# A gated attention and GLU mix in split fp32: one stock of buffers, and a new seam between its two phases

## The chip, the core and the metric

The kernel is one program on one core of a Trainium2 chip. The metric is the device time of one execution in microseconds (us), as the median of several runs; lower is better. The engines that matter are TensorE (PE in the profile, with its weight loads as PEld), VectorE (DVE), ScalarE (ACT), GpSimd (POOL, which here issues DMAs that add to what lies in the target) and SyncE (SP, which issues the plain DMAs).

## The reference, cut to what matters

x has 2048 rows of 512 columns. A sigmoid gate per row mixes two branches: linear attention with 32 heads of 16, and a bilinear GLU with 1792 hidden columns. All of it is fp32.

```
x = A_x                                              # [2048, 512]
g = sigmoid((x * gate_w).sum(-1))                    # one number per row
q, k, v = split(x @ wqkv);  phi(t) = where(t > 0, t + 1, exp(t)) + 1e-6
kv  = einsum("bhsd,bhse->bhde", phi(k), v);  z = phi(k).sum(over rows)
num = einsum("bhqd,bhde->bhqe", phi(q), kv)
den = einsum("bhqd,bhd->bhq", phi(q), z) + 1e-6
a = (num / den) @ wo
b = ((x @ w_gate) * (x @ w_up)) @ w_down
out = g * a + (1 - g) * b
```

## The kernel before, in words

**Arithmetic.** Every fp32 operand is held as two parts, a high one in the type fp32r and a low one (operand minus high). A product is three matmuls, high by high, high by low and low by high (`mm3`, L72). The high part is a copy on ACT, the low part a subtraction on DVE.

**Phase 1** (L171 to L348) goes over 16 tiles of 128 rows. For a tile t it computes k (12 matmuls into the bank `pk`), phi(k) on ACT and DVE (`phi_k`, `phi_split`), splits x (`split_x`, which also sums x times `gate_w` into a column of `scol`), and adds x-transposed times phi(k) into four banks `gt` (12 matmuls, `g_unit`), four tiles behind the k products. So the loop has 12 turns with both kinds of products and, at its end, four with g products alone. The sum over rows of phi(k) gathers in `zacc`. After the last turn come the gates: a sigmoid on a 128 x 16 column tile gives `gcol` (g) and `ocol` (1 - g), which two DMAs write to DRAM in turned order, one element at a time (L341), and from where they are read later as rows: g by eight loads (`g2_load`, L767), 1 - g in the last group of each half (`row`, L498). In this phase the loop also loads and splits the sums of x blocks that phase 2 needs (`cb_load`), and the weights of the first units. Its buffers come from a pool of its own (`p1`), with a fixed count for each kind.

**Phase 2** works on two halves of 1024 rows (`pair`). A half has 16 **units** of seven products each: two q units and 14 f units (gate and up columns of the GLU). A unit multiplies four weight blocks by blocks of x with seven products in place of eight: sums of weight blocks and sums of x blocks are formed first, and the seven results are combined through four PSUM banks Y, X, R, S by ACT and DVE (`crit`, L599). One product is six matmuls of 512 columns. It has a **slot**: slot 7n+s is the product s of unit n, and everything else is put down against slots (`later(slot, fn)`). Two f units make a **group** (7 per half). Beginning 11 slots after its first one, a group's products with w_down run as 14 **jobs** of three matmuls each, one to a slot, behind the unit's product. They run in banks `pdn`, of which there are four, and are gathered in SBUF tiles `M`: every other job has its bank loaded beforehand with the old sum by ACT (`seed`) and evacuated by ACT, the rest are added by DVE. The last group of a half is plain, and its jobs and the attention's last products run in `turn` behind the half's last unit, and in the first slots of the next half (`FILL`).

**Weights.** `w_load(n)` loads five of a unit's seven weight blocks (640 KB) by SP when the unit n-3 is emitted; `w_add(n)` fills the last two from the first two with the sign turned, on ACT, and then a DMA of POOL adds five more blocks to blocks 2 to 6; `w_high` and `w_low` split the result. `d_load`, `d_add`, `d_high` and `d_low` do the same for a group's w_down. The ACT copy in `w_add` and `d_add` waits for the load, and what stands behind it on ACT waits with it.

**The seam.** At the end of phase 1 SP has, in order, the two gate stores, eight loads for attention (`wp_load`: w_v and w_o, 256 KB each), the eight g loads, and only then the first w_down load. Of the units the q ones come first, at slots 0 to 13. The term kv is made at slot 9 (`kv_unit`) from the `gt` banks, which ACT and DVE have copied out ahead of slot 0 (`g_evac`).

**Order.** Every instruction is pinned in the order in which the code emits it, engine by engine. An engine, SP and POOL too, takes its instructions in that order and holds at the first whose wait isn't over. Phase 2's 512-column tiles come from one stock of 45 buffers (`get`, L357, takes the one that was given back longest ago; `put` gives back).

Of the kernel before, what the change touches and what calls it, by code (L numbers as in the profile page):

```python
# [7 lines left out]
F32 = mybir.dt.float32  # L8
# [6 lines left out]
P = 128  # L15
S = 2048
D = 512
# [18 lines left out]
SLOT = {3: 0, 4: 1, 5: 2, 2: 3, 1: 4, 6: 5, 7: 6}  # L36
# [5 lines left out]
def gated_mix(ctx: ExitStack, tc, xt, xp, x, wqkv, wq, wq_add, wo, wgu, wgu_add, wdn, wdn_add, gate_w, out):  # L42
# [48 lines left out]
    gcol = const.tile([P, NT], F32, name="gcol")  # L91
    ocol = const.tile([P, NT], F32, name="ocol")
# [24 lines left out]
    gates = [dram.tile([NT, P], F32, name=f"gate{v}") for v in "go"]  # L117


    order = [("q", j) for j in range(2)] + [("f", f) for f in range(NF)]  # L120
    units = len(order)
    order = [(pair, *u) for pair in range(NPAIR) for u in order]
# [4 lines left out]
    def w_load(n):  # L127

        if n < len(order):
            _, kind, m = order[n]  # L130
            raws[n] = const.tile([P, 7, 2 * P], F32, tag="wr", name="wr", bufs=2)
            dma(raws[n][:, 0:5], (wgu if kind == "f" else wq)[m])

    def w_add(n):

        if n < len(order):
            _, kind, m = order[n]
            act(raws[n][:, 5:7], raws[n][:, 0:2], scale=-1.0)
            dma_add(raws[n][:, 2:7], (wgu_add if kind == "f" else wq_add)[m])

    PARTS = ((0, 2), (2, 4), (4, 7))
# [27 lines left out]


    accs = [psum.tile([P, D], F32, tag="pd", name=f"gt{d}", bufs=4) for d in range(KT)]  # L171
    with tc.tile_pool(name="p1", bufs=2, reuse_waits="tile") as p1:

        warm = psum.tile([P, CH], F32, tag="Y", name="warm")
        for _ in range(WARM):
            mm(warm, zeros[:, :P], zeros, start=True, stop=True)
        gw = p1.tile([P, D], F32, name="gw", bufs=1)
        zacc = p1.tile([P, D], F32, name="zacc", bufs=1)
        nc.vector.memset(zacc, 0.0)
        wkh = p1.tile([P, KT, D], F32R, name="wkh", bufs=1)  # L180
        wkl = p1.tile([P, KT, D], F32R, name="wkl", bufs=1)

        xop = {}
        for t in range(2 * CH // P):
            c, i = divmod(t, CH // P)
            xop[t] = [part[:, :, i * P:(i + 1) * P] for part in (xa, xb)[c]]


        raw_of = [p1.tile([P, D], F32, tag="raw", name="wraw", bufs=4) for _ in range(KT)]

        def raw_load(k, by):
            pin(by.dma_start(raw_of[k], wqkv[k * P:(k + 1) * P, D:2 * D]))

        raw_load(0, nc.scalar)
        for k in range(KT):
            raw = raw_of[k]
            a = p1.tile([P, LEAD, P], F32, tag="xtraw", name="xlead", bufs=4)
            step = LEAD // 2 if k == 0 else LEAD
            for i in range(0, LEAD, step):
                sl = slice(i * P, (i + step) * P)  # L200
                dma(a[:, i:i + step].rearrange("p t c -> p (t c)"), xp[0, A1 + k // 2][:, k % 2, sl])
                if i + step == LEAD and k + 1 < KT:
                    raw_load(k + 1, nc.sync)
                if i == 0:
                    act(wkh[:, k], raw)
                split(xa[0][:, k, sl], xa[1][:, k, sl], a[:, i:i + step].rearrange("p t c -> p (t c)"), "dve")
                if i == 0:
                    tt(wkl[:, k], raw, wkh[:, k].bitcast(F32), ALU.subtract)

        xs, xts, pks = {}, {}, {}  # L210

        def load_x(t):
            xs[t] = p1.tile([P, D], F32, tag="raw", name="xraw", bufs=4)
            dma(xs[t], x[t * P:(t + 1) * P, :])

        def load_xt(t):
            xts[t] = p1.tile([P, KT, P], F32, tag="xtraw", name="xtraw", bufs=4)
            dma(xts[t], xt[t])

        def split_xt(t):  # L220
            if t not in xop:
                xop[t] = [p1.tile([P, KT, P], F32R, tag=f"xt{v}", name=f"xt{v}", bufs=3) for v in "hl"]
            split(*xop[t], xts.pop(t))

        def k_mm(pk, t, k, **kw):
            mm3(pk, [v[:, k] for v in xop[t]], (wkh[:, k], wkl[:, k]), k == 0, k == KT - 1, late=1, **kw)

        def phi_k(t, pk):

            e = p1.tile([P, D], F32, tag="e", name="e")  # L230
            r = p1.tile([P, D], F32, tag="u", name="r")
            act(e, pk, AF.Exp)
            act(r, pk, AF.Relu)
            ph = p1.tile([P, D], F32, tag="ph", name="ph")
            stt(ph, e, 1.0, r, ALU.min, ALU.add)
            return t, ph

        def phi_split(t, ph):
            pkh = p1.tile([P, D], F32R, tag="pkh", name="pkh", bufs=4)
            pkl = p1.tile([P, D], F32R, tag="pkl", name="pkl", bufs=4)  # L240
# [23 lines left out]
        for t in range(1, 3):  # L264
            load_x(t)
            load_xt(LEAD + t)
# [752 lines left out]
```

## Time and profile before

| | |
|---|---|
| median of 3 runs | 643.28 us (642.03 to 646.67) |
| profiled execution, its own time | 644.63 us |
| its span, first to last instruction | 642.8 us |
| PE busy | 596.3 us (93%), 2579 matmuls |
| DVE busy | 507.0 us (79%) |
| ACT busy | 398.2 us (62%) |
| POOL busy | 57.0 us (9%) |
| moved by DMA | 107.35 MB, 167 GB/s on average |

A line of the profile that groups instructions gives the line of code, the engine, the operation, the tile written and those read, and the count. `L50` is the line of every matmul, `L56` of every ACT operation that goes through `act`, `L59` and `L62` of DVE's, `L80` of SP's DMAs and `L83` of POOL's, so tiles tell them apart. The chain of waits is followed back from the last instruction to what released each step. A row of the view by windows gives a stretch of time, its length, and for PE, PEld, DVE, ACT and POOL the busy time and the count of instructions, then the TensorE clock that was granted, the busy share of the DMA engines and their rate.

### The profile page before, as it was taken

Reading aid. Unit: us, or ns where it says so; the run is one execution under the profiler, and the core shown is the slowest. Engines: PE = TensorE matmul, PEld = TensorE weight load, DVE = VectorE, ACT = ScalarE, POOL = GpSimd, SP = SyncE. Lnnn points to the kernel's source line nnn. Section 1 sums busy time; section 2 is a strip of 40 time slices with the busy share of each in tenths; the row PEclk is TensorE's granted clock in tenths of the full one; section 3 lists DMA queues with packets and bytes.
Section 4 is the critical chain, followed back from the end, with each engine's and each line's share of the span. In section 5 each row is a group of like instructions: output and inputs, shape, how many; then the busy total and the mean of one; then the engine's idle time right before and its main releaser. Section 6 shows DMA issues by size and latency. Waiting matters only on the chain.

```text
span 642.8 us, 7716 instructions
## 1 busy us (share of the span) xinstructions
PE 596.3 (93%) x2579; PEld 483.4 (75%) x2579; DVE 507.0 (79%) x813; ACT 398.2 (62%) x707; POOL 57.0 (9%) x74
## 2 busy tenths in 40 slices
PE   8999995089799899999999879999999999999997
PEld 6888884078578688878887768867878888888776
DVE  6977874048699698988898885699989888889881
ACT  3756743159468587777776265666867777677410
POOL 0011100000101111112100011000101010000000
PEclk9999999589999899999999999999999999999999
DMA  8576928769967778889757626898757375660011
GB/s 296 184 198 163 256 42 36 226 132 285 255 153 217 156 221 202 216 200 229 180 140 238 214 68 150 227 248 210 209 141 164 91 158 140 144 139 19 0 66 66
DMA packets 46680, 107.35 MB, mean 167 GB/s; under 512 B 8080, under 2 KB 17296, under 8 KB 46608
## 3 DMA queue, kind: packets, MB, share of 16 engines
q1 hardware_dynamic: 37360, 70.41, 35.0%
q0 software_dynamic: 9136, 36.18, 30.2%
q8 instruction: 20, 0.33, 0.2%
q10 hardware_dynamic: 144, 0.26, 0.1%
q14 instruction: 20, 0.16, 0.1%
HBM read 95.55 MB, written 12.34 MB: 168 GB/s over the span
## 4 chain that ended last, share of the span: by engine, by line
PE 64%; DMA 17%; DVE 12%; ACT 3%; issue 3%; SPq 0%; DVEq 0%; ACTq 0%; POOL 0%; POOLq 0%
PE pdn L50 18%; PE bY L50 10%; PE bR L50 9%; PE bX L50 8%; PE pk L50 7%; PE gt L50 6%; PE bS L50 5%; DMA dr<-in_wdn 5%; DVE M L59 4%; DMA wr<-in_wgu 4%; DMA gateo<-ocol 3%; DMA xw<-in_xp 2%; DMA wo_sb<-in_wo 2%; DMA wr<-in_wgu_add 1%; DVE wcl L59 1%
## 5 line engine op out<-in xcount | busy, mean ns | idle before, releaser
L56 ACT ACTIVATE M<-pdn 128x512 f32<-128x512 f32 x98 | 58.6, 598 | 38.4 <-PE pdn L50 35.6
L50 PE MATMUL pdn<-hh,dh 128*128 128x512 f32 x200 | 78.4, 392 | 4.4 <-ACT pdn L56 4.4
L50 PE MATMUL pdn<-hl,dh 128*128 128x512 f32 x200 | 78.5, 393 | 3.6 <-DVE hl L59 3.6
L59 DVE TENSOR_TENSOR M<-M,pdn 128x512 f32<-128x512 f32 x86 | 58.9, 685 | 26.5 <-PE pdn L50 26.4
L50 PE MATMUL pdn<-hh,dl 128*128 128x512 f32 x200 | 78.3, 392 | 0.0
L59 DVE TENSOR_TENSOR wcl<-wr,wch 128x512 fp32r<-128x512 f32 (+1 forms) x96 | 74.3, 775 | 1.8 <-ACT wch L56 1.7
L56 ACT ACTIVATE wch<-wr 128x512 fp32r<-128x512 f32 (+1 forms) x96 | 66.9, 701 | 2.0 <-DMA wr<-in_wgu_add 1.9
L50 PE MATMUL bX<-xbh,wch 128*128 128x512 f32 x128 | 49.9, 390 | 0.0
L50 PE MATMUL bX<-xbh,wcl 128*128 128x512 f32 x128 | 49.8, 389 | 0.0
L50 PE MATMUL bX<-xbl,wch 128*128 128x512 f32 x128 | 49.8, 389 | 0.0
L83 POOL DMA_DIRECT2D wr<-in_wgu_add x28 | 24.7, 881 | 273.3 <-ACT wr L56 125.1
L50 PEld LDWEIGHTS pdn<-hh,dh 128*128 128x128 f32 x200 | 37.7, 188 | 13.4 <-ACT pdn L56 5.6
L50 PEld LDWEIGHTS pdn<-hl,dh 128*128 128x128 f32 x200 | 37.8, 189 | 12.5 <-DVE hl L59 4.8
L50 PE MATMUL bY<-xc4h,wch 128*128 128x512 f32 x64 | 26.4, 412 | 22.2 <-ACT m L56 22.2
L59 DVE TENSOR_TENSOR bR<-bX,m 128x512 f32<-128x512 f32 x32 | 22.3, 696 | 29.5 <-ACT m L56 21.9
L50 PEld LDWEIGHTS pdn<-hh,dl 128*128 128x128 f32 x200 | 37.7, 188 | 7.8
L56 ACT ACTIVATE pdn<-M 128x512 f32<-128x512 f32 x70 | 41.7, 596 | 0.0
L56 ACT ACTIVATE hh<-c 128x512 fp32r<-128x512 f32 x56 | 35.1, 626 | 9.2 <-DVE c L59 9.2
L59 DVE TENSOR_TENSOR hl<-c,hh 128x512 fp32r<-128x512 f32 x56 | 38.4, 686 | 2.5 <-ACT hh L56 2.4
L59 DVE TENSOR_TENSOR t<-bR,c 128x512 f32<-128x512 f32 x32 | 22.0, 687 | 17.3 <-PE bR L50 13.5
L56 ACT ACTIVATE c<-bX 128x512 f32<-128x512 f32 x28 | 16.8, 598 | 28.2 <-DVE bS L59 26.8
L50 PEld LDWEIGHTS bY<-xc4h,wch 128*128 128x128 f32 x64 | 12.5, 196 | 26.5 <-ACT m L56 24.0
(178 smaller groups left out, 1554.7 us busy)
## 6 DMA issues: line engine op xcount, KB each, us to landing
wr<-in_wgu SPq DMA_DIRECT2D x28, 640.0 KB
wr<-in_wgu_add POOLq DMA_DIRECT2D x28, 640.0 KB, 7.8
dr<-in_wdn SPq DMA_DIRECT2D x14, 640.0 KB
dr<-in_wdn_add POOLq DMA_DIRECT2D x12, 640.0 KB, 9.0
xraw<-in_x SPq DMA_DIRECT2D x16, 256.0 KB
terms<-zq SPq DMA_DIRECT2D x16, 256.0 KB
zt<-terms SPq DMA_DIRECT2D x16, 256.0 KB
rb<-den SPq DMA_DIRECT2D x16, 256.0 KB
```

What stands on the lines that cost most here:

```text
L50: tc.keep_in_program_order(nc.tensor.matmul(*args, **kw))
L56: pin(nc.scalar.activation(dst, src, func, **kw))
L59: pin(nc.vector.tensor_tensor(dst, a, b, op=op))
L83: tc.keep_in_program_order(nc.gpsimd.dma_start(dst, src, accum_op=ALU.add))
```

## The change

- **One stock.** Phase 1 takes all its tiles from the stock of 45 that phase 2 uses, and its pool is gone. The x block sums are loaded, added to and split in halves of 512 columns (ten in place of five), and from tile 4 on in place of tile 6.
- **The last g products.** The loop ends with tile 15's k products. The 16 pieces of three matmuls that remain (`g_piece`, tiles 12 to 15) stand in a queue, from which slots 0 to 13 take one each, slots 3 and 9 two. What they need (phi of the last two tiles, three splits of x), the sum of `zacc` and the gates are put down at slots 0 to 9. `g_evac` moves to slot 15, `kv_unit` from 9 to 16.
- **The gates.** g and 1 - g stand in one tile of 32 columns, which DVE turns in blocks of 32 x 32; four DMAs store rows of 32 elements.
- **The q units.** The second one comes behind the first group: q0, f0, f1, q1, f2 and so on. Its chain for the denominators has slots of its own (`ZAT`).
- **The weights.** A load brings three blocks (384 KB) in place of five. ACT fills four more with two copies, one with the sign turned and one of block 11 twice, and POOL's DMA adds five blocks as before. The plain group's w_down has a load of its own with four blocks. The order of blocks and parts changes with it.
- **SP's order at the seam.** The first w_down load goes ahead of the loads for attention, which go to slot 4; the g loads go to slot 14. The x sums of the second half start at slot 51 in place of 40 and hold their buffers for 10 slots in place of 15.

In the rows below, `wr` is a unit's raw weights, `dr` a group's, `wv` and `wo_sb` the attention's, `xraw` a tile of x, `terms` and `zt` what the denominators write and read, `g_` the g rows. SP at the seam, before:

```order
L80 DMA wr<-in_wgu 128x1280
L80 DMA gateg<-gcol 128x16x1
L80 DMA gateo<-ocol 128x16x1
L80 DMA wv<-in_wqkv 128x512 x4
L80 DMA wo_sb<-in_wo 128x512 x4
L80 DMA g_982<-gateg 32x1x128 x8
L80 DMA dr<-in_wdn 128x1280
L80 DMA wr<-in_wgu 128x1280
L80 DMA terms_1007<-zq 128x4x128 x4
```

And SP at the same place in the changed kernel:

```order
L80 DMA wr<-in_wgu 128x768
L80 DMA xraw<-in_x 128x512
L80 DMA dr<-in_wdn 128x768
L80 DMA wv<-in_wqkv 128x512 x4
L80 DMA wo_sb<-in_wo 128x512 x4
L80 DMA wr<-in_wq 128x768
L80 DMA terms_897<-zq 128x4x128 x2
L80 DMA gates<-turned 32x32 x4
L80 DMA terms_897<-zq 128x4x128 x2
L80 DMA wr<-in_wgu 128x768
L80 DMA g_896<-gates 32x1x128 x8
L80 DMA zt<-terms_897 128x512 x4
```

The first `dr` load stood behind both gate stores and the eight g loads, and stands ahead of them now; the weight rows are 768 elements wide in place of 1280.

PE where the units begin, before (`gt` the g banks, `pz` the sum of `zacc`, `bY` and `bX` a unit's banks):

```order
L50 MATMUL gt_92<-pkh,xnh 128x512
L50 MATMUL gt_92<-pkl,xnh 128x512
L50 MATMUL gt_92<-pkh,xnl 128x512
L50 MATMUL pz<-ones,zacc 128x2 x4
L50 MATMUL bY<-xah,wch 128x512
L50 MATMUL bY<-xal,wch 128x512
L50 MATMUL bY<-xah,wcl 128x512
```

PE between the first two products of the first unit, in the changed kernel:

```order
L50 MATMUL bY<-xah,wch 128x512
L50 MATMUL bY<-xal,wch 128x512
L50 MATMUL bY<-xah,wcl 128x512
L50 MATMUL gt_90<-pkh,xnh 128x512
L50 MATMUL gt_90<-pkl,xnh 128x512
L50 MATMUL gt_90<-pkh,xnl 128x512
L50 MATMUL bX<-xbh,wch 128x512
```

A g piece stands between two products where there was none; PE has 2535 rows in both programs.

ACT in an f unit of the dense part, around the fill of a unit's raw weights, before (`pdn<-M` is a seed):

```order
L56 ACTIVATE wch<-wr 128x768
L56 ACTIVATE wr<-wr 128x512
L56 ACTIVATE M<-pdn 128x512
L56 ACTIVATE xw<-xw 128x512
L56 ACTIVATE wch<-wr 128x512
L56 ACTIVATE pdn<-M 128x512
```

And in the changed kernel:

```order
L56 ACTIVATE xw<-xw 128x512
L56 ACTIVATE wr<-wr 128x512 x2
L56 ACTIVATE pdn<-M 128x512
L56 ACTIVATE wch<-wr 128x512
L56 ACTIVATE c_2203<-bX 128x512
```

The fill is two instructions in place of one, ahead of the next seed.

The diff, cut to its core:

```diff
-SLOT = {3: 0, 4: 1, 5: 2, 2: 3, 1: 4, 6: 5, 7: 6}
+SLOT = {3: 0, 4: 1, 2: 2, 6: 3, 7: 4, 5: 5, 1: 6}
...
-    order = [("q", j) for j in range(2)] + [("f", f) for f in range(NF)]
+    order = [("f", f) for f in range(NF)]
+    for j, place in enumerate((0, 3)):
+        order.insert(place, ("q", j))
...
-            dma(raws[n][:, 0:5], (wgu if kind == "f" else wq)[m])
+            dma(raws[n][:, 0:3], (wgu if kind == "f" else wq)[m])
+
+    def copies(raw):
+
+        act(raw[:, 3:5], raw[:, 0:2], scale=-1.0)
+        act(raw[:, 5:7], raw[:, 0:1].to_broadcast([P, 2, 2 * P]))
...
-            act(raws[n][:, 5:7], raws[n][:, 0:2], scale=-1.0)
+            copies(raws[n])
             dma_add(raws[n][:, 2:7], (wgu_add if kind == "f" else wq_add)[m])
 
-    PARTS = ((0, 2), (2, 4), (4, 7))
+    PARTS = ((0, 3), (5, 7), (3, 5))
...
-        for there, col in zip(gates, (gcol, ocol)):
-            dma(there.rearrange("t p -> p t"), col)
+        pin(nc.vector.transpose(rows, both))
+        for a in range(0, P, 2 * NT):
+            dma(gates[:, a:a + 2 * NT], rows[a:a + 2 * NT])
...
+    later(0, phi_rest)
+    later(2, phi_rest)
+    for t, s in zip(range(NT - LEAD + 1, NT), (1, 4, 7)):
+        later(s, lambda t=t: split_x(t))
+    later(5, z_sums)
+    later(9, gate)
+    queue += [lambda t=t, d=d: g_piece(t, d) for t in range(NT - LEAD, NT) for d in range(KT)]
...
-            dma(draw[g][:, 0:5], wdn[g % NG])
+            if g % NG < NG - 1:
+                dma(draw[g][:, 0:3], wdn[g % NG])
+            else:
+                dma(draw[g][:, 0:4], wdl)
...
-            act(draw[g][:, 5:7], draw[g][:, 0:2], scale=-1.0)
+            copies(draw[g])
             dma_add(draw[g][:, 2:7], wdn_add[g % NG])
...
-    FILL = {}
+    FILL = {s: 1 + (s in (3, 9)) for s in range(14)}
...
+    ZAT = ((15, (21, 23, 24), 26, 28), (24, (31, 33, 35), 37, 40))
...
-    g_evac()
-    later(0, g2_load)
-    later(9, kv_unit)
-    later(11, kv_split)
+    later(14, g2_load)
+    later(15, g_evac)
+    later(16, kv_unit)
+    later(18, kv_split)
...
-        later(40 + 5 * n, lambda i=i, k=k: x_raw(i, k))
-        later(43 + 5 * n, lambda i=i, k=k: x_sum(i, k))
+        later(51 + 5 * n, lambda i=i, k=k: x_raw(i, k))
+        later(54 + 5 * n, lambda i=i, k=k: x_sum(i, k))
...
-    later(7, lambda: d_add(0))
-    wp_load()
+    later(4, lambda: d_add(0))
+    later(4, wp_load)
```

397 lines of the change are left out of this document (206 added, 191 removed).

## The prediction

> **What bounds the kernel now.** I read the page first, for the engines and the chain that ended last.
>
> ```profile
> PE 596.3 (93%) x2579; PEld 483.4 (75%) x2579; DVE 507.0 (79%) x813; ACT 398.2 (62%) x707; POOL 57.0 (9%) x74
> PE 64%; DMA 17%; DVE 12%; ACT 3%; issue 3%; SPq 0%; DVEq 0%; ACTq 0%; POOL 0%; POOLq 0%
> ```
>
> PE's share hides what the time goes to, since a matmul that waits or runs at a lower clock counts as busy too. So I take the pace from a row of the chain, and count matmuls by stretches.
>
> ```profile
> 62.46 2.72 PE gt L50 x12
> ```
>
> Twelve in 2.72 us is 0.2267 us each. Rows of the view by windows, with cuts where the slices of the page change:
>
> ```profile
> 5.00:92.20 87.20, 87.20 (x384) 72.21 (x385) 71.31 (x131) 53.90 (x92) 6.28 (x7) 1.00 0.69 199
> 92.20:163.00 70.80, 46.72 (x206) 37.50 (x204) 31.96 (x51) 35.05 (x62) 3.46 (x4) 0.83 0.76 165
> 163.00:222.00 59.00, 52.18 (x210) 41.11 (x211) 48.53 (x80) 37.19 (x68) 6.93 (x8) 0.94 0.76 193
> 222.00:344.00 122.00, 121.67 (x537) 100.48 (x536) 108.02 (x167) 92.33 (x169) 16.51 (x19) 1.00 0.80 198
> 344.00:386.00 42.00, 36.15 (x154) 28.25 (x154) 36.66 (x54) 19.60 (x30) 5.41 (x8) 1.00 0.55 165
> 420.00:474.00 54.00, 51.51 (x221) 40.73 (x220) 52.60 (x85) 39.00 (x72) 5.19 (x6) 1.00 0.77 209
> 474.00:600.00 126.00, 126.00 (x557) 104.30 (x557) 111.14 (x173) 92.26 (x170) 8.65 (x10) 1.00 0.53 120
> 600.00:642.80 42.80, 37.57 (x162) 29.61 (x160) 25.39 (x41) 5.94 (x10) 0.00 (x0) 1.00 0.13 50
> ```
>
> Count times 0.2267 fills phase 1 (384: 87.1 of 87.2 us) and both long stretches of f units (537: 121.7 of 122.0; 557: 126 of 126). There PE is the bound and nothing is to be had. Of the 206 in the seam's stretch, 32 belong to kv and 8 to the z sums:
>
> ```profile
> 92.22 0.95 PE L50 MATMUL pz<-ones,zacc 128*128 128x2 f32 x8
> ...
> 130.51 4.12 PE pkv L50 x32
> ```
>
> So 166 x 0.2267 + 4.1 + 0.9 = 42.7 of 70.8 us, and **28.1 us are lost**. In the same way 163 to 222 loses 59.0 - 47.6 = **11.4**, 344 to 386 loses 42.0 - 34.9 = **7.1**, 420 to 474 loses 54.0 - 50.1 = **3.9**, the end 42.8 - 36.7 = 6.1. Who is waited for stands in the waits of PE and ACT and in the chain:
>
> ```profile
> PE bY L50 <- ACT m L56: 22.2, 2, 21.8
> ...
> ACT dr L56 <- DMA dr<-in_wdn: 35.4, 6, 21.5
> ...
> ACT wr L56 <- DMA wr<-in_wgu: 10.2, 4, 4.1
> ```
>
> ```profile
> 91.12 20.66 DMA gateo<-ocol
> 111.80 9.72 DMA wo_sb<-in_wo
> 122.17 4.23 DMA dr<-in_wdn
> ...
> 164.35 8.29 DMA dr<-in_wdn
> ...
> 201.78 13.37 DMA wr<-in_wgu
> ```
>
> At the seam the gate store takes 20.66 us; SP holds behind it, the first w_down load goes out at 122.17, and ACT stands at that load's sign copy with the evacuation `m` behind it, for which PE waits 21.8 us. The clock adds to it (0.83 over the stretch). The later losses begin with a weight load, too.
>
> **The change part by part.** PE's matmuls stay as they are, so I move losses only. Costs of an ACT and a DVE instruction are taken from the dense stretch 222 to 344: 92.33 / 169 = 0.55 us and 108.02 / 167 = 0.65 us.
>
> *The seam.* The first w_down load goes ahead of everything that waits for gates, and the element-wise stores are gone: the wait of 21.8 us has no cause left. What is late next? Slots 0 to 13 hold 132 matmuls (7 x 12 of the units, 16 x 3 of g), 29.9 us of PE; counted from the order, ACT has 39 instructions (21.5 us) and DVE 36 (23.4 us). In the first seven slots it is tight: PE 66, 15.0 us; ACT 25, 13.7 us; DVE 21, 13.6 us. Each g piece's operands are made two slots or more (4 us) ahead of it. Slots 14 to 31: 162 matmuls and kv, 40.8 us; ACT 67, 36.9 us; DVE 56, 36.4 us. The z sums need `zacc` of slot 2 at slot 5, and `kv_unit` the `gt` copies of slot 15 at slot 16: both behind PE work of their slot (1.36 us), and kv itself gives 4.1 us to catch up. What first units lose without a gate wait is bounded by two rows: the dense stretch, 0.3 us, and the same units once the wait was over:
>
> ```profile
> 127.50:163.00 35.50, 33.11 (x143) 26.74 (x143) 23.70 (x37) 25.38 (x45) 2.44 (x3) 0.89 0.77 210
> ```
>
> 143 less 32 is 111, 25.2 us, and 4.1 for kv: 6.2 of 35.5 us lost, with a clock still low. I take 2, near the lower end, since the clock never falls first: **28.1 to 2, a gain of 26.1**.
>
> *The gates themselves.* Off PE's path: ACT's exponential and DVE's four small instructions at slot 9. The turn on DVE isn't in the trace; it lies between the small and the large ones of the old gate code and `g_evac`, 0.25 to 0.68 us, and I take 0.25, for 32 columns are nearer to 16 than to 512. The new store isn't either:
>
> ```profile
> L339 DVE RECIPROCAL gcol<-gcol 128x16 f32<-128x16 f32 x1 | 0.3, 254 | 0.0
> L718 DVE COPY gts<-gt 128x512 f32<-128x512 f32 x2 | 1.3, 682 | 0.0
> ```
>
> ```profile
> SPq L80 <- DMA den<-den: 9.3, 2, 5.6
> ```
>
> SP held 5.6 us at most for the small `den` store and 20.66 passed for the old gates; I take 5.6, as both new and `den` stores move rows and not single elements. SP holds for DVE at slot 9, then for this landing ahead of the g loads; behind it wait `zt`, a weight load and the second `dr`. `zt` is used at slot 21, so 5.6 us are covered by slots 14 to 20 (15.5 us with kv).
>
> *Shorter loads, two copies.* A load has 0.6 of its bytes. If its time goes with them, 8.29 becomes 5.0 and 13.37 becomes 8.0. ACT's waits at these two loads:
>
> ```profile
> 172.72 0.63 ACT L56 ACTIVATE dr<-dr 128x512 f32<-128x512 f32 x1 [5.48 <-DMA dr<-in_wdn]
> ```
>
> ```profile
> 215.18 0.63 ACT L56 ACTIVATE wr<-wr 128x512 f32<-128x512 f32 x1 [4.12 <-DMA wr<-in_wgu]
> ```
>
> ```profile
> 170.00:180.00 10.00, 6.70 (x23) 4.81 (x22) 6.13 (x11) 6.78 (x14) 0.87 (x1) 0.83 0.93 221
> 210.00:220.00 10.00, 6.89 (x25) 5.23 (x24) 5.55 (x9) 5.58 (x10) 0.87 (x1) 0.84 0.69 153
> ```
>
> These two windows lose 10 - 5.2 and 10 - 5.7, 9.1 of the stretch's 11.4 us. The first load had 2.8 us until ACT came; now it is issued in slot 16 and wanted in slot 19, with kv between (up to 8.9 us), so its wait goes. The second had 13.37 - 4.12 = 9.25; the three slots ahead of it lose their jobs (the second group's begin at slot 39), 3 x 0.68 us, and leave 7.2: a load of 8.0 is waited for 0.8 us. These slots, 32 to 38, are lean: PE 42 matmuls, 9.5 us, ACT 16, 8.8 us, DVE 16, 10.4 us, so another 1 us. With the 2.3 us that lay elsewhere: **11.4 to 4, a gain of 7.4**. Bounds: 0.5, and 10.8 if nothing shortens (2.3 + 13.37 - 7.2, and 2.3 for the first).
>
> The Trainium skill's page "DMA: Bandwidth & Descriptors", in "Anatomy of one DMA — SWDGE (gpsimd) path", gives a transfer about 2.0 us fixed plus its bytes at 436 GB/s (fitted on POOL's path): by it a load goes from 3.5 to 2.9 us, and an estimate of the stretch would keep 10.6, a kernel of 615 us. The two rows took 8.29 and 13.37 us, with the DMA engines 0.93 and 0.69 busy: mostly queueing, which bytes of all loads set.
>
> The price is on ACT: the second copy isn't in the trace, the first has
>
> ```profile
> L56 ACT ACTIVATE wr<-wr 128x512 f32<-128x512 f32 x32 | 20.1, 629 | 10.2 <-DMA wr<-in_wgu 10.2
> ```
>
> with the same elements out: 0.55 to 0.63 us, 44 times (32 units, 12 groups), 24 us. In the dense stretch ACT rises from 76% (92.33 / 122) by 13 x 0.55 = 7 us to 81%, beside PE. Seeds stand behind the copies, and POOL's add goes 0.55 us later. PE waited for seeds 4.4 us in all:
>
> ```profile
> PE pdn L50 <- ACT pdn L56: 4.4, 3, 3.1
> ```
>
> I take **1 us lost**; bounds 0 and as many again, 4.4. If the cover were gone, all 24.
>
> *The half's end, second half.*
>
> ```profile
> 347.62 10.57 DMA dr<-in_wdn
> 360.09 9.16 DVE M L59 x16
> ...
> 459.94 11.19 DMA wr<-in_wgu
> ```
>
> The first stands behind seven x loads of 0.52 MB, which stay, as do the DVE sums; two weight loads bring 0.52 MB less of 5.0 in all, a tenth, 1.1 us of 10.57: 7.1 to 6, a gain of 1.1 (bounds 0 and 4.2, 0.4 of the row). For the third, 0.6 of 11.19 is 4.5 us shorter, more than any of ACT's waits on it (4.1): 3.9 to 2.5, a gain of 1.4 (0 to 3.4).
>
> *At nothing:* w_v and w_o at slot 4 for slots 16 and 19 (24 us of slots); x sums 11 slots later, still off SP before slot 105; x splits in halves, ten on DVE in place of five of double size, in tiles 9 to 15, where DVE has 54 x 0.65 = 35 us and PE 168 x 0.2267 = 38; the second q unit's chain in slots 31 to 40, where DVE has 0.65 x 214 = 139 of 145.5 us over slots 39 to 110. If that cover fails it is part of the 4.4 above.
>
> **Sum.** 642.8 - 26.1 - 7.4 - 1.1 - 1.4 + 1 = 607.8 us of span. The profiled execution took 644.63, 1.83 over its span and 1.35 over the median 643.28; so the median should be 607.8 + 0.5 = **608 us**. With the largest unknown, the stretch of the two loads, at its bounds it is 604 to 615.
>
> **Rivals.**
> *Nothing new is late.* Seam, two loads and second half at their lower bounds, no loss to copies: 642.8 - 27.8 - 10.9 - 1.1 - 3.4 + 0.5 = 600. For it: three engines fit into every slot range but one. Against: at 0.9 full they rarely do so without a wait.
> *The waits move to the second group's loads.* A load's time doesn't go with its bytes: slots 14 to 40 now hold both the g and `zt` traffic, two DRAM copies and three weight loads close together. Seam 6.2, next stretch 10.8, nothing at the half's end or later, copies 2: 642.8 - 21.9 - 0.6 + 2 + 0.5 = 623. For it: the DMA share of 0.93. Against: 44 loads with 0.26 MB less each. The skill's fixed cost is a weaker form of it.
> *The new gate store is no faster than the old.* Units begin at 92.2 - 48 x 0.2267 = 81.3 us, slot 9 ends at 103; 20.66 us, and 5.6 each for the landings of g and `zt`, make 135. DVE's z sums at slot 21 (128 us) wait 7 us: 615. Against: 128 runs of 32 elements in place of 4096 single ones.
> *Slower: phase 1 starves on the common stock.* SP takes a buffer for tile t+3 in turn t; if it comes back too late, SP holds, and every load of the phase behind it. Twelve turns of 5.44 us; a load is wanted 16.3 us after its turn. To eat the 35 us gained and 6 more, each turn must lose 3.4 us, so buffers must come back 20 us late, nearly four turns. Against: by count of the code 12 of 45 are free at the tightest, about a turn's takings, and DVE, which gives back last, has work for 71.31 of 87.2 us. Price then: 650.
>
> **Chances.** Forecast 0.67, nothing late 0.10, moved waits 0.14, slow gate store 0.04, starvation 0.05 (0.03 of it over the line). The range 599 to 621 takes the forecast with its bounds, the slow store and the case that nothing is late (0.81); the moved waits lie just above it. About 1% (6.4 us) is what a measurement can tell from no change: faster 0.95, same 0.02, slower 0.03.
>
> **What would show it.** Right: no PE gap over 3 us between 80 and 160 us, clock 1.00 there; SP's first `dr` ahead of `wv`; the gate store under 6 us; `wr` loads of 5 to 8 us and ACT waits for them under 3 us in all; dense stretches still at 0.2267 us; ACT near 81% in them. Wrong: ACT waiting for `dr` or `wr` in slots 19 to 22 and 38 by more than 3 us each, a low clock after it, DVE waiting for `zt`, SP holding in phase 1.

## The result, and the profile after

The changed kernel took **618.61 us** (median, 616.07 to 619.59), beside 644.97 (642.03 to 650.57) for the kernel before on the same chip: a ratio of 0.9575 with a 95% interval of 0.9499 to 0.9651. A second measurement with more runs, told below, gave 0.9613 (0.9578 to 0.9648). So the change is worth 4%; the forecast of 608 us was 10.6 us too low, and the range 599 to 621 holds the time. The profiled execution took 617.82 us with a span of 616.1. One slow execution, of the run with the w_o products later (1202.77 us, nearly twice its others), is left out of that run's ratio.

From the page of the kernel after, the busy times and the chain that ended last:

```profile
PE 594.6 (97%) x2579; PEld 480.5 (78%) x2579; DVE 505.1 (82%) x819; ACT 419.1 (68%) x758; POOL 61.0 (10%) x79
...
PE 66%; DVE 16%; DMA 9%; ACT 4%; issue 4%; SPq 0%; DVEq 0%; ACTq 0%; POOLq 0%
```

ACT has 21 us more to do (the copies), DVE no more than before. The share of DMA in the chain has halved, from 17 to 9%. Where the matmuls lose time is counted as in the prediction, 0.2267 us each, from rows of the view by windows (window, length, then busy time and count for PE, PEld, DVE, ACT and POOL, the granted clock, the DMA engines' share and their rate):

```profile
81.20:137.00 55.80, 53.88 (x256) 44.40 (x254) 37.23 (x65) 36.78 (x68) 4.29 (x5) 1.00 0.73 185
137.00:190.00 53.00, 50.16 (x209) 40.01 (x210) 44.47 (x71) 42.19 (x78) 4.29 (x5) 0.97 0.64 149
190.00:210.00 20.00, 20.00 (x89) 16.54 (x89) 18.42 (x31) 16.02 (x30) 2.58 (x3) 1.00 0.61 148
210.00:256.00 46.00, 41.52 (x174) 31.78 (x173) 37.70 (x60) 32.27 (x61) 7.77 (x9) 1.00 0.82 187
256.00:307.00 51.00, 51.00 (x226) 42.24 (x225) 44.70 (x69) 41.59 (x77) 6.89 (x8) 1.00 0.75 180
307.00:360.00 53.00, 48.63 (x202) 38.36 (x201) 47.57 (x73) 29.20 (x49) 6.24 (x9) 0.97 0.61 164
...
420.00:480.00 60.00, 59.33 (x257) 47.47 (x256) 55.38 (x89) 46.84 (x86) 5.18 (x6) 1.00 0.70 155
480.00:570.00 90.00, 89.76 (x395) 73.65 (x394) 81.94 (x129) 70.38 (x131) 6.05 (x7) 1.00 0.45 100
570.00:616.10 46.10, 40.61 (x175) 32.11 (x173) 28.36 (x46) 6.99 (x12) 0.00 (x0) 1.00 0.12 46
```

The first row holds the z sums and kv, whose 40 small matmuls stand in the chain:

```profile
93.80 0.79 PE pz L50 x8
...
116.52 3.67 PE pkv L50 x32
```

So the seam loses 55.80 - 216 x 0.2267 - 3.67 - 0.79 = 2.4 us, and the others likewise:

| part of the program | lost before, us | forecast | lost after |
|---|---|---|---|
| seam (first units; 92 to 163 before, 81 to 137 after) | 28.1 | 2 | 2.4 |
| the next slots (163 to 222; 137 to 190) | 11.4 | 4 | 5.6 |
| the f units behind them (222 to 344; 190 to 307) | 0.3 | 0.3 and 1 for copies | 6.6, all of it between 210 and 256 |
| the half's end (344 to 386; 307 to 360) | 7.1 | 6 | 7.2 |
| second half (420 to 474; 420 to 570) | 3.9 | 2.5 | 2.2 |
| the end | 6.1 | 6.1 | 6.4 |

The sums are 56.9 and 30.4, a gain of 26.5, and the spans differ by 26.7. The seam came out as forecast. The span is 8.3 us over the forecast 607.8, and 5.3 of them (6.6 less the 0.3 and 1 that were allowed) lie in a stretch that had lost nothing. What it waits for stands in the waits of the whole execution, and in the chain inside that stretch:

```profile
DVE phq L62 <- DMA rb<-den: 11.1, 8, 3.7
...
ACT dr L56 <- DMA dr<-in_wdn: 3.6, 1, 3.6
...
ACT wr L56 <- DMA wr<-in_wgu: 1.2, 2, 0.7
```

```profile
216.73 9.64 DMA rb<-den
...
227.75 1.66 PE bR L50 x6
...
230.79 11.21 DMA rb<-den
242.03 0.70 DVE phq L62
...
242.80 0.61 ACT m L56
...
243.45 1.66 PE bY L50 x6
```

`rb` is one over the denominator (times g), spread over the heads' rows: `norm` loads it, `scale` multiplies phi(q) by it on DVE. DVE meets these loads before they have landed (11.1 us in all, 6.3 of them between 210 and 256 us, and 2.0 before the change); behind DVE stand the evacuations of the units, and behind those PE. ACT's waits for weights, which the change set out from, are down from 45.6 us to 4.8.

### The profile page after: what moved, and what is told of

It is laid out like the page before. It is cut to its first block, busy times and chain, and to the rows that moved or that the text cites. A ratio compares the mean times of both kernels' runs of the same rounds, so it can differ in the third digit from the quotient of the medians.

```text
span 616.1 us, 7802 instructions
## 1 busy us (share of the span) xinstructions
PE 594.6 (97%) x2579; PEld 480.5 (78%) x2579; DVE 505.1 (82%) x819; ACT 419.1 (68%) x758; POOL 61.0 (10%) x79
## 2 busy tenths in 40 slices
DMA packets 44185, 95.56 MB, mean 155 GB/s; under 512 B 4304, under 2 KB 13520, under 8 KB 44112
## 4 chain that ended last, share of the span: by engine, by line
PE 66%; DVE 16%; DMA 9%; ACT 4%; issue 4%; SPq 0%; DVEq 0%; ACTq 0%; POOLq 0%
PE pdn L50 18%; PE bY L50 10%; PE bR L50 10%; PE bX L50 9%; PE pk L50 7%; PE gt L50 7%; DVE M L59 5%; DMA rb<-den 5%; PE bS L50 4%; DVE wcl L59 2%; DVE hl L59 2%; DVE c L59 2%; DMA dr<-in_wdn 2%; DMA wr<-in_wgu_add 1%; DVE t L59 1%
## 5 line engine op out<-in xcount | busy, mean ns | idle before, releaser
L56 ACT ACTIVATE wr<-wr 128x512 f32<-128x512 f32 x64 | 36.8, 628 | 1.2 <-DMA wr<-in_wgu 1.2
L56 ACT ACTIVATE m<-bY 128x512 f32<-128x512 f32 x32 | 19.1, 598 | 19.0 <-PE bY L50 15.0
L59 DVE TENSOR_TENSOR dl<-dr,dh 128x512 fp32r<-128x512 f32 (+1 forms) x40 | 29.6, 766 | 2.0 <-ACT dh L56 1.8
```

The source lines that it names most:

```text
L56: pin(nc.scalar.activation(dst, src, func, **kw))
L59: pin(nc.vector.tensor_tensor(dst, a, b, op=op))
```

## The experiments

Ratios are to the kernel before, run beside each kernel on the same chip. Kernels of different groups of runs are compared by these ratios, times 642 us; for the kernel after, the ratio of the second measurement, 0.9613, is taken. By the intervals such a difference is good to 4 or 5 us.

### One part alone: the order on SP

The kernel before, with the loads of g behind the first w_down load:

```
-    later(0, g2_load)
     later(9, kv_unit)
...
     later(0, lambda: d_load(0))
+    later(0, g2_load)
```

> The kernel before, with one thing moved: the first w_down load is queued on SP ahead of the eight loads that read the gates back, not behind them. The element-wise gate stores, the emptied end of phase 1 and the order of the q units stay. Theory A (the seam's 28.1 us were that queue: SP held for the 20.66 us store with the load behind it, ACT at the load, PE at ACT): the load goes out near 95 us in place of 122, PE's wait of 21.8 us is gone, and the kernel takes 645 - 20 to 24 = 621 to 625 us. Rival B (phase 1's emptied end and the crowded start of phase 2 cost most of it, and another wait steps in): 632 us or more, with the seam's stretch still losing over 14 us.

639.82 us, ratio 0.9949 (0.9920 to 0.9979): 3 us, where 20 to 24 were expected. The load stands ahead of the g loads now, and yet goes out at 112.42 us, not near 95, and lands at 122.6. The chain of this kernel, and its DMA engines in the ten microseconds concerned:

```profile
92.89 19.51 DMA wv<-in_wqkv
...
112.42 10.19 DMA dr<-in_wdn
...
123.26 0.49 ACT m L56
```

```profile
100.00:110.00 10.00, 6.59 (x29) 4.84 (x27) 5.70 (x9) 4.62 (x9) 0.00 (x0) 0.97 0.98 45
```

The DMA engines are full (0.98) and move 45 GB/s while the store of 2 x 2048 single elements is on its way, and a w_v load issued behind it takes 19.51 us. SP holds as well. In this trace its DMAs report to eight landing semaphores in turn, and from the third w_o load on each goes out only when the eighth DMA before it on SP has landed: the w_down load at 112.42, as the first w_v load has landed (92.89 + 19.51 = 112.40), and the fourth w_o load at 111.96, as the store's second half has (111.95). So the run moved the load by some 10 us on SP, but did not free SP from the store, and theory A's order (the load ahead of the store itself) is not what it tested. Rival B's number held (632 us or more); its reason, phase 1's emptied end, isn't what the trace shows.

### One part alone: the gates turned on DVE

The kernel before, with the new way to store the gates and nothing else; the core of the edit:

```
-        for there, col in zip(gates, (gcol, ocol)):
-            dma(there.rearrange("t p -> p t"), col)
+        rows = p1.tile([P, 2 * NT], F32, name="turned", bufs=1)
+        pin(nc.vector.transpose(rows, both))
+        for a in range(0, P, 2 * NT):
+            dma(both_rows[:, a:a + 2 * NT], rows[a:a + 2 * NT])
```

> The kernel before, with only its gate stores replaced by the turn on DVE and four stores of rows; the order of SP's loads, phase 1's emptied end and everything else stay as before. Moving a load ahead of the wait (the run with the g loads behind the first w_down load) gained 3 us only: there the w_v load took 19.51 us and the w_down load 10.19 behind it, with the DMA engines 0.97 busy at 44 GB/s. Theory A (the element-wise store itself fills the DMA engines, whatever SP's order): with it gone the w_down load lands before 105 us, PE's wait of 17 to 22 us falls under 5, the clock stays up, and the kernel takes 618 to 626 us, most of what the whole change gives. Rival B (the seam is lost to phase 1's emptied end, or to the eight 256 KB loads ahead of the first w_down load): 633 us or more.

627.38 us, ratio 0.9758 (0.9697 to 0.9819): 15.5 us of the 25 or so that the whole change brings, by four lines. The same ten microseconds, and the chain:

```profile
100.00:110.00 10.00, 6.01 (x26) 4.38 (x24) 5.12 (x8) 4.04 (x8) 0.00 (x0) 0.91 0.75 202
```

```profile
96.84 9.36 DMA wo_sb<-in_wo
...
106.84 3.74 DMA dr<-in_wdn
```

202 GB/s in place of 45. PE's wait is 5.8 us in place of 21.8; what is left of it hangs on the eight 256 KB loads that still stand ahead of the w_down load, which lands at 110.6 us and not before 105. The time lies just above the expected 618 to 626. Without the store both SP's hold behind it and the full DMA engines are gone, so this run alone doesn't tell them apart.

### One part undone: the old gate store in the kernel after

```
-        turned = get("turned")
...
-        for a in range(0, P, 2 * NT):
-            dma(gates[:, a:a + 2 * NT], rows[a:a + 2 * NT])
+        for there, col in ((gates[0:NT], gcol), (gates[NT:2 * NT], ocol)):
+            dma(there.rearrange("t p -> p t"), col)
```

> The kernel after, with the two element-wise gate stores of before in place of the turn on DVE and four stores of rows. Theory A (what a slow store costs now is what still stands behind the gate loads on SP: the denominators' loads, the second w_down load, a weight load): SP holds some 12 us longer at slot 14, ACT stands at the second w_down load in slot 19, and 5 to 10 us are lost: 624 to 629 us. Rival B (with the first w_down load ahead of it, the store is covered; the turn was worth nothing by itself): 617 to 621 us.

632.45 us, ratio 0.9826 (0.9763 to 0.9888): 13.7 us more than the kernel after, above even theory A's 5 to 10.

```profile
110.00:120.00 10.00, 10.00 (x62) 8.87 (x61) 7.76 (x12) 4.74 (x9) 0.00 (x0) 1.00 1.38 26
```

```profile
111.18 17.74 DMA wr<-in_wgu
...
131.50 8.99 DMA dr<-in_wdn
```

```profile
DMA packets 48121, 95.56 MB, mean 151 GB/s; under 512 B 8240, under 2 KB 17456, under 8 KB 48048
```

The packets below 512 bytes number 8240, where the kernel after has 4304: some 4000 more, about one for each element. While they run the engines count as more than full (1.38) and move 26 GB/s. A weight load caught among them takes 17.74 us, and here SP didn't hold it back: in the kernel after it goes out at 111.14 us, 0.04 sooner, and takes 3.72. Theory A counted only the loads that SP holds back; those already out are slowed as well.

### The second chain earlier

```
-    ZAT = ((15, (21, 23, 24), 26, 28), (24, (31, 33, 35), 37, 40))
+    ZAT = ((15, (21, 23, 24), 26, 28), (15, (21, 23, 24), 26, 28))
...
-            later(T + first + 3 + 3 * k, lambda r=r, c=c: scale(r, c))
+            later(T + first + (4, 4)[j] + 3 * k, lambda r=r, c=c: scale(r, c))
```

> The kernel after, with the second q unit's denominator chain nine slots earlier (its loads in slot 36, not 45, its scalings from slot 53, not 64), and each scaling four slots behind its rb load in place of three. Theory A (the 6.6 us lost between 210 and 256 us are DVE at those rb loads, which it meets too early, and ACT at the x loads that share the DMA engines with them): the wait for rb falls from 11.1 us to under 3, that stretch loses 2 us or less, 613 to 615 us. Rival B (DVE is simply full there, at 37.7 us of 46, and the work comes due earlier in slots 32 to 46, where there is no more room): the loss moves forward to 160 to 200 us, 617 to 621 us.

629.77 us, ratio 0.9793 (0.9743 to 0.9844): 11.6 us slower than the kernel after, worse than both theories. PE stands 5.5 us at 180 us and 4.5 at 441. SP's own waits from 150 to 180 us, and the chain:

```profile
SPq L80 <- DMA terms<-zq: 5.6, 1, 5.6
```

```profile
175.49 8.81 DMA rb<-den
```

In slot 36 SP now takes the four `zt` loads, which must wait for the last `terms` store to land; behind them stand a w_down load and the first unit's last `rb` load. That load goes out at 175.49 and DVE waits 7.6 us for it, and ACT waits 6.3 us for the w_down load just ahead. So what makes `rb` late at this place is not DVE's fullness but what stands ahead on SP. That became the next theory.

### The w_o products later

```
-        later((19, 20, 22, 24)[b], lambda b=b: wo_split(b))
-        later((22, 24, 26, 28)[b], lambda b=b: wp_unit(b))
+        later((27, 28, 29, 30)[b], lambda b=b: wo_split(b))
+        later((29, 32, 33, 35)[b], lambda b=b: wp_unit(b))
```

> The kernel after, with the four w_o splits and the four products of w_o with kv in slots 27 to 35 in place of 19 to 28. Theory A (in slots 21 to 27 ACT and DVE have as much work as PE, so PE waits there, 5.4 us between 119 and 150 us with the low clock that follows): the stretch loses 2 us or less, 614 to 616 us. Rival B (the cause is the chain through kv at slots 16 to 18, or the first weights' arrival): the same 5 us at the same place, 617 to 621 us.

Ratio 0.9650 (0.9587 to 0.9713), not to be told from the kernel after, and a span of 615.8 us. Theory A is right on the place and wrong on the total:

```profile
81.20:137.00 55.80, 55.80 (x266) 46.63 (x265) 39.91 (x70) 39.10 (x73) 5.15 (x6) 1.00 0.76 190
...
150.00:180.00 30.00, 22.12 (x91) 17.02 (x90) 20.51 (x33) 18.86 (x35) 2.57 (x3) 0.97 0.68 158
```

By 137 us ten more matmuls are done (266 for 256), which is all the seam had lost. Then 150 to 180 us loses 30 - 91 x 0.2267 = 9.4 us:

```profile
165.28 1.22 DVE dl L59 x2
...
166.51 0.34 SPq L80
...
166.94 8.54 DMA rb<-den
...
175.51 0.07 DVE phq L62
```

Here the new theory shows in four lines. The w_down load of slot 37 needs the one buffer `dr`, which DVE gives back with `dl`. SP holds at it; once it is free SP issues that load and then the `rb` load behind it, which needed nothing, and DVE meets that one three slots later. The time won in slots 22 to 28 was waited away here.

### The w_down loads two slots later

```
-            when(9, lambda: d_load(g + 1))
-            when(12, lambda: d_add(g + 1))
+            when(11, lambda: d_load(g + 1))
+            when(15, lambda: d_add(g + 1))
```

> The kernel after, with each group's next w_down load put down two slots later (11 for 9 after the group's start) and the copies and the add three slots later (15 for 12). Theory A (the load waits on SP for its one buffer, which DVE gives back with dl in slot 9 of the group; the rb load behind it went out 10 us after the one ahead, at 170.24, 230.79 and 428.09 us, and DVE then met it too early): DVE's wait for rb falls from 11.1 to 6 us or less, 613 to 616 us. Rival B (rb is late because its load takes 8 to 11 us beside other transfers, whenever it goes out): the wait stays at 9 us or more, 617 to 621 us.

612.55 us, ratio 0.9537 (0.9484 to 0.9590): 4.9 us less than the kernel after by the ratios, a little faster than expected. DVE's wait for `rb`, from the waits of this kernel, falls from 11.1 to 3.4 us:

```profile
DVE phq L62 <- DMA rb<-den: 3.4, 4, 1.5
```

From its windows, the stretch that lost 6.6 us:

```profile
208.00:252.00 44.00, 41.29 (x176) 32.33 (x175) 38.48 (x62) 33.85 (x63) 8.64 (x10) 1.00 0.83 192
```

It loses 44 - 39.9 = 4.1 us. The load moved costs nothing where it now lies. Rival B falls by its number (a wait of 9 us or more), but only half by its reason. The first q unit's last `rb` load, in slot 37, goes out at 164.32 us in place of 170.24: that is SP's order. The second unit's four, between 208 and 252 us, go out at 217.19, 221.73, 229.68 and 234.78, where the kernel after has 216.73, 220.91, 230.79 and 235.00. There SP's order changed by 1.1 us at most; the loads themselves took less, 7.4 to 9.0 us in place of 8.1 to 12.8. Since 4.1 us are still lost with little wait for `rb`, it is not the whole cause there.

### Three moves, and the x sums later

The next two runs add up: first the w_o products later and the w_down loads later, by the two diffs above, and the first unit's scalings five slots behind their loads:

```
-            later(T + first + 3 + 3 * k, lambda r=r, c=c: scale(r, c))
+            later(T + first + (5, 3)[j] + 3 * k, lambda r=r, c=c: scale(r, c))
```

> The kernel after with three moves: the w_o splits and products in slots 27 to 35, the w_down loads two slots later, and the first q unit's four scalings five slots behind their rb loads in place of three (the second unit's stay at three, since the stock of 45 has no buffer left there). The w_o move alone took away the loss between 119 and 150 us, and as much was lost again at rb between 159 and 180. Theory A (both losses are order, not load: w_o's packed slots, then rb behind the w_down load on SP): both stretches lose 3 us together in place of 6.7, 609 to 613 us. Rival B (what is won early is lost to the next late transfer, since the DMA engines are what bounds slots 14 to 75): 616 to 621 us.

611.89 us, ratio 0.9535 (0.9472 to 0.9598): inside theory A's band, but no better than the w_down loads alone by the ratio (the span, 609.0 us, is 2.5 less).

The scalings of the second unit could not be moved likewise: with one stock of 45, counting what is taken and given back slot by slot, nothing is left there while the x sums hold their tiles. So the second run puts the x sums elsewhere:

```
-        later(51 + 5 * n, lambda i=i, k=k: x_raw(i, k))
...
+        later(70 + 3 * n, lambda i=i, k=k: x_raw(i, k))
...
-            later(T + first + 3 + 3 * k, lambda r=r, c=c: scale(r, c))
+            later(T + first + (5, 5)[j] + 3 * k, lambda r=r, c=c: scale(r, c))
```

> As the run with three moves, and besides the x sums from slot 70 on, one in three slots, in place of slot 51 on, one in five; this frees buffers, so that both q units' scalings stand five slots behind their rb loads. Theory A (the stretch 210 to 256 us lost its 6.6 us at rb loads and x loads that share the DMA engines): that stretch loses 1 us or less, and the x sums at 250 to 320 us cost under 2: 604 to 609 us. Rival B (ten x sums in 30 slots in place of 50 make the loads there late): 250 to 320 us, which lost nothing, loses 4 us or more: 612 us or more.

609.96 us (609.15 to 610.66), ratio 0.9496 (0.9444 to 0.9548): just above theory A's upper edge of 609. No wait for `rb` is left, and the denser x sums cost nothing that the trace shows.

```profile
208.00:252.00 44.00, 43.65 (x190) 35.21 (x190) 40.35 (x64) 35.39 (x67) 6.00 (x7) 1.00 0.73 165
```

The stretch that lost 6.6 us loses 44 - 190 x 0.2267 = 0.9, as theory A expected. The second unit's `rb` loads take 4.8 to 5.5 us to land, where they took 7.1 to 8.7 in the run with three moves, which differs in the x sums and in the second unit's scalings alone, and 8.1 to 12.8 in the kernel after. The third still goes out right behind a w_down load (225.53 after 225.16). So it was the x loads beside them that made them long; the later scalings leave them two slots more.

### One part undone: five blocks per load

The kernel after, with block 11's copies loaded again, for w_down likewise, and with the order of blocks and parts that belongs to it; the core of the edit:

```
-            dma(raws[n][:, 0:3], (wgu if kind == "f" else wq)[m])
+            dma(raws[n][:, 0:5], (wgu if kind == "f" else wq)[m])
...
-        act(raw[:, 3:5], raw[:, 0:2], scale=-1.0)
-        act(raw[:, 5:7], raw[:, 0:1].to_broadcast([P, 2, 2 * P]))
+        act(raw[:, 5:7], raw[:, 0:2], scale=-1.0)
```

> The kernel after, with block 11's two copies loaded again and not made by ACT: five blocks per load (640 KB in place of 384), one ACT copy in place of two, the add as before. Theory A (the prediction's terms: shorter loads gave 7.4 us in the stretch of slots 18 to 38, 1.1 at the half's end and 1.4 later, the copies cost 1): undone, ACT waits for w_gu and w_down loads by 5 us or more again and the kernel takes 6 to 9 us more than the one after. Rival B (the loads' new places in the queue gave that gain, not their size, and ACT is now fuller than the DMA engines): within 2 us of the one after, with ACT's share at 63 to 65%, or faster.

626.21 us, ratio 0.9739 (0.9707 to 0.9771), 8.4 us more than the kernel after in the same group of runs. The prediction's terms for this part sum to 7.4 + 1.1 + 1.4 - 1 = 8.9. The waits that differ most:

```profile
DVE phq L62 <- DMA rb<-den: 13.3, 7, 4.3
...
PE pdn L50 <- ACT pdn L56: 9.3, 7, 3.7
ACT xw L56 <- DMA xw<-in_xp: 8.4, 2, 4.2
ACT dr L56 <- DMA dr<-in_wdn: 7.4, 5, 3.9
...
ACT wr L56 <- DMA wr<-in_wgu: 2.0, 4, 0.7
```

The size was right, the place was not. The longer `wr` loads themselves are hardly waited for (2.0 us, 1.2 in the kernel after). It is mostly w_down loads (7.4, after 3.6), the x sums' loads (8.4, after 2.9) and `rb` that are late. Two rows of this run, for the matmuls that the kernel after has in 137 to 190 and in 190 to 210 us:

```profile
139.90:192.10 52.20, 48.70 (x210) 38.61 (x209) 43.54 (x70) 39.01 (x72) 3.43 (x4) 1.00 0.69 172
192.10:216.30 24.20, 21.59 (x89) 17.48 (x88) 19.43 (x32) 16.45 (x30) 2.57 (x3) 0.93 0.70 175
```

They lose 4.6 and 4.0 us, where the kernel after loses 5.6 and nothing. So the stretch to which the prediction gave 7.4 of its 8.9 us loses no more with long loads than with short ones. The bytes count ahead of it (the seam, 81.5 to 139.9 us here, loses 4.8 us in place of 2.4) and behind it.

### The second q unit ahead of the first group, and the kernel after again

```
-    for j, place in enumerate((0, 3)):
+    for j, place in enumerate((0, 1)):
...
-    ZAT = ((15, (21, 23, 24), 26, 28), (24, (31, 33, 35), 37, 40))
+    ZAT = ((15, (21, 23, 24), 26, 28), (15, (21, 23, 24), 26, 28))
```

> The kernel after, with the second q unit directly behind the first again (ahead of the first group), and its denominator chain at the first one's distances. Theory A (the place behind a group pushed the second chain into slots 45 to 73, where PE has no slack, and cost the 6.6 us lost there): the stretch of those slots loses 2 us or less, slots 7 to 13 hold the added work, and the kernel takes 3 to 6 us less than the one after. Rival B (two chains within seven slots pile up on DVE in slots 21 to 31, where it then has 24 us of work against 22 on PE, and rb loads stand behind each other on SP): 2 us or more slower than the one after.

> The kernel after once more, unchanged, beside the three runs it is compared with: a narrower interval for its ratio to before, 0.953 to 0.961, if the first measurement holds.

The kernel after: 617.83 us, 0.9613 (0.9578 to 0.9648), at the upper edge of what was expected. With the q units together: **610.86 us**, ratio 0.9508 (0.9475 to 0.9542), 7.0 us less, theory A and a little more.

One line of its waits and one of its windows:

```profile
DVE phq L62 <- DMA rb<-den: 1.9, 3, 1.0
```

```profile
137.00:250.00 113.00, 111.27 (x486) 90.68 (x487) 103.95 (x166) 88.79 (x165) 14.63 (x17) 1.00 0.73 167
```

From 137 to 250 us it loses 113 - 486 x 0.2267 = 2.8 us; the kernel after lost 5.6 + 6.6 from 137 to 256. So this part of the change made the kernel slower than it would have been with the rest alone. In the kernel after, the second chain's loads (slots 45 to 70) lie among the loads of the x sums (from slot 51 on); with the q units together they are out by slot 44, and `rb` is hardly waited for, though each scaling still stands three slots behind its load.

### The best version

As the run with the x sums later, and with three rows of slots chosen anew:

```
-        later((27, 28, 29, 30)[b], lambda b=b: wo_split(b))
-        later((29, 32, 33, 35)[b], lambda b=b: wp_unit(b))
+        later((19, 26, 28, 29)[b], lambda b=b: wo_split(b))
+        later((29, 32, 34, 38)[b], lambda b=b: wp_unit(b))
...
-            later(T + first + (5, 5)[j] + 3 * k, lambda r=r, c=c: scale(r, c))
+            later(T + first + (6, 5)[j] + 3 * k, lambda r=r, c=c: scale(r, c))
```

> As the run with three moves and the x sums from slot 70, with three slots chosen anew: w_o splits in 19, 26, 28 and 29, products in 29, 32, 34 and 38, and the first q unit's scalings six slots behind their loads. Theory A (the 4.4 us still lost between 159 and 166 us are ACT and DVE, which have a little more work than PE in the jobless slots 32 to 38): that stretch loses 2 us, 607 to 609 us. Rival B (the fixed order of sums and splits that begins at slot 35 costs it, whatever else is moved): 609 to 611 us, the same gaps.

**606.64 us** (605.70 to 607.53), ratio 0.9436 (0.9403 to 0.9469), 11.2 us less than the kernel after in the same group. From 137 to 190 us, 222 matmuls in place of 209:

```profile
137.00:190.00 53.00, 50.89 (x222) 41.05 (x221) 45.29 (x73) 44.32 (x83) 3.44 (x4) 1.00 0.69 167
```

That is 53 - 50.3 = 2.7 us lost, and the time lies just below theory A's 607. Whether the q units' old order adds to this version wasn't tried.

## Why the prediction was right, and where it was 10 us off

- **The seam, 28.1 to 2: right in size (2.4), half right in cause.** The prediction read the 21.8 us as SP holding behind the gate store. The chain shows that hold, but moving the load past the g loads alone gained only 3 us. What the prediction left out is that the store's own packets fill the DMA engines and slow every load beside them. Taking the store away alone gave 15.5 us, putting it back cost 13.7, so the store is the main cause; how much of it is SP's hold and how much the slowed loads was not separated, since no run put the load ahead of the store with all else as before. The queue matters once the store is gone, too: PE's last 5.8 us there (the run with the gates alone) hang on the loads ahead of the first w_down load, which the change also puts behind it.
- **The new gate store: right.** The turn took 0.21 us (0.25 was taken). The four stores land 1.3 to 1.4 us after they go out, where 5.6 was taken, and no wait of SP for them is in the trace. The rival that priced a slow store at 615, 7 us over the forecast, had half its price: 13.7 us were measured, since the store also slowed the loads that were already out.

```profile
L409 DVE STREAM_TRANSPOSE turned<-both 128x32 f32<-128x32 f32 x1 | 0.2, 211 | 0.0
```

- **Shorter loads, 11.4 to 4: 5.6 came out, and the part as a whole is worth 8.4 us by the undoing, where 8.9 were forecast; but that the two agree is luck.** With five blocks per load and the rest as in the kernel after, this stretch loses 4.6 us: what took it from 11.4 to 5.6 is not the size of the loads, and which other part of the change did it was not run. The bytes pay where the prediction put nothing, in 190 to 210 us (4.0) and in the seam (2.4). ACT's waits at `wr` of 10.2 and at `dr` of 35.4 us (21.5 of them the seam's) are down to 1.2 and 3.6. The Trainium skill's page "DMA: Bandwidth & Descriptors", section "Anatomy of one DMA — SWDGE (gpsimd) path", gives a fixed 2.0 us and the bytes at 436 GB/s, by which the forecast kept a case of 615 with little gain from shorter loads. In the kernel after the 384 KB loads of unit weights took 3.0 to 12.1 us; 2.9 by an estimate from the page's figures, so it fits the quickest. The 8.4 us speak against using it alone where loads queue: most of what came back is waits at other loads.
- **The copies, 1 us: nothing seen.** In 256 to 307 us ACT is busy 41.59 of 51 us, 82% where 81 was forecast, and 226 matmuls fill the stretch without a loss.
- **The half's end and the second half: 7.2 for 6, and 2.2 for 2.5.** The w_down load at the half's end took 9.85 us in place of 10.57, near the tenth that was forecast. What the forecast lacked there is the clock: it stood at half for 3.4 us from 346.9 us on, 1.7 us of matmuls, where it was at 1.00 before the change.
- **The step that failed: "at nothing: ... the second q unit's chain in slots 31 to 40".** These slots count from the unit's first, 21; the loads stand in slots 45 to 70 and the scalings in 64 to 73. The cover was counted in DVE's instructions (139 of 145.5 us), and there was room for them. What wasn't counted was the chain's loads. A scaling stood four slots behind its `rb` load before the change and three after, which is 6.1 us at 27 matmuls to three slots. The four loads went out 0.9 us after their slots began at the latest, but took 8.1 to 12.8 us to land beside the x sums' loads (9.64 and 11.21 in the chain above). That cost 6.6 us in a stretch forecast dense, more than the 4.4 that the prediction allowed for. With the x sums later and the scalings five slots behind, 0.9 of the 6.6 is left.
- **A smaller miss of the same kind:** for slots 14 to 31 the prediction summed ACT (36.9 us) and DVE (36.4) against PE's 40.8. Slots 22 to 25 alone hold 21 ACT and 20 DVE instructions, 11.6 and 13.0 us at the prediction's rates, beside 9.5 us of PE. An average over 18 slots hid a knot in four. Moving w_o out of it freed those slots, but not the kernel, until the w_down loads no longer held up `rb` on SP.
- **What would show it:** right on the PE gaps up to 160 us (the longest 2.5 us), on the order of the first `dr` and `wv`, on the gate store (under 6 us), on ACT's waits for `wr`, on ACT's share. Wrong on the clock, which fell to half for 3.4 us at 145 us, on the `wr` loads (3.0 to 12.1 us, half of them under 4.6, and not 5 to 8), and on the dense stretch. The case that nothing is late (600) was not reached, but the best version came to within 7 us of it by order alone (606.64).
- **What stays open:** undone alone, the turn costs 13.7 us and the short loads 8.4, and the second q unit's place gains 7.0, 15.1 of the change's 24.8 us if they add. The rest (phase 1's end filled with g pieces in the one stock, the place of the first w_down load) was not undone by itself.

## What to carry to other kernels

Before moving a chain of work to a place that looks empty, count its loads as well as its instructions: what stands ahead of each on the issuing queue, what that one waits for, what else moves beside it, and how many slots the reader leaves it. A wait in the chain names who was last, not why a load was slow: look at the DMA engines' rate beside their share, and let a store of single elements at high share and low rate be the first suspect. After a large gain, undo each part alone; here one of them, the q unit's new place, cost 7 us that the others paid for. And look where the undoing costs, not only how much: the short loads gave the forecast sum in other places than forecast.

## What was not expected of the hardware

Single-element DMA packets block far more than their own bytes: with 4096 of them on their way, 16 KB in all, the DMA engines moved 26 to 45 GB/s at a share of 0.98 to 1.38, and loads of 256 and 384 KB took 17.7 to 19.5 us.

The clock fell after shorter pauses than expected. In the kernel after PE paused for 2.50 us between two starts at 141.66 us, and from 145.50 on ran 3.4 us at half clock:

```profile
141.66:145.50 3.84, 1.73 (x8) 1.10 (x7) 3.29 (x6) 2.01 (x4) 0.00 (x0) 1.00 0.23 45
145.50:148.90 3.40, 3.40 (x10) 2.59 (x9) 3.37 (x8) 0.83 (x2) 0.00 (x0) 0.50 0.00 0
```

The same happened at 346.9 us, behind a pause of 2.15 us at 343.8. A pause of 2.36 us at 237 us left it at 1.00, as the row for 210 to 256 above shows, and so did one of 2.62 us at 162.7 in the run with three moves. So the length of the last pause alone doesn't tell. The Trainium skill's page "TensorE: Matmul & The Clock Gate", section "Why this matters for your kernels", asks for no idle gaps over about 3 us; here 2.50 and 2.15 us from start to start were enough.
